# Pooling the 16-row tails of v once per batch on 128 partitions, in place of once per group on 32

## The chip, the cores and the metric

The kernel runs on one core of one Trainium2 chip. The metric is the device time of one execution in microseconds (us). The engines are TensorE (PE in the views, its weight loads PEld), VectorE (DVE), ScalarE (ACT), GpSimd (POOL) and SyncE (SP), which issues nearly all DMAs.

## What is computed

Three stages follow each other: an attention whose keys and values are means over 8 neighbouring rows, and two feed-forward layers. Cut to what matters:

```python
B, H, S, D = 8, 8, 576, 64
k_p = k.reshape(B, H, 72, 8, D).mean(axis=3)
v_p = v.reshape(B, H, 72, 8, D).mean(axis=3)
scores = q @ k_p.T / sqrt(D)                  # per batch and head
attn   = softmax(scores)                      # over the 72 pooled keys
x  = (attn @ v_p) as [B*S, H*D] = [4608, 512]
x  = ((x @ w1) * (x @ w2)) @ w3 @ w_out       # first layer, 1024 wide
h  = x @ w_in;  out = (h * sigmoid(1.702 * h)) @ w_out2   # second, 2048 wide
```

Everything is float32. A float32 product is made of three fast ones: each operand is split into a rounded part and a rest (a cast on ScalarE, a subtraction on VectorE or GpSimd).

## The kernel before

**Groups.** The attention is cut into 32 groups, four for each batch; a group is two heads. Its pooled v has 2 x 72 = 144 rows, 16 more than the 128 partitions. The first 128 rows go through a tile on 128 partitions (`vr`, `va`, `vf`, `vm`), and the 16 left over, the last rows of the group's second head, through tiles on 32 partitions (`vtr`, `vat`, `vtf`, `vt`). These are the tails. `v_load` (L243) issues both DMAs of a group, `g_va` (L318) pools both by three halving additions each on GpSimd and scales them (L332 for the tail; `mask` also sorts the 128 rows into the two heads), and at its end calls `v_load` for the next group. `g_vb` (L336) splits both: `vm` by one cast on ScalarE and one subtraction on GpSimd, `vt` by two casts (L340, L341) and one subtraction (L342). `vt` holds rounded part, rest, rounded part in three blocks of 32 partitions. `g6` multiplies `vm` and `vt` by the split probabilities and writes the result, split again, into the slots of `x`.

**What runs beside it.** `g0` to `g4` load and turn q and k, make the scores and the softmax, and split the probabilities (L369, L372 on GpSimd). `tick` issues the next part of the attention; the first four groups go through `tick_first`. `conv.step` converts a weight tile from the input's 64-bit floats: two ScalarE instructions (L166, L168), a shift on VectorE (L169), an addition on GpSimd (L172), and then a split (L105). There are 40 such tiles for the first layer. The weights `w3` are multiplied with `w_out` beforehand (`w3_mm`, L508 turns them).

**Order.** First a loop of 28 steps (L568) does conversions, the product of `w3` and `w_out`, and the attention of the first four groups. Then come nine blocks of 512 rows (L602): each of eight steps of a block multiplies by `w1` and `w2`, takes the product (L641), splits it, and calls `tick` twice, so that one block carries four groups. The blocks' matmuls and those of the second layer fill the rest. Tiles are allocated from pools; `vr` has one buffer, so its next load has to wait until the old one has been read last. The order in each engine's queue is not the order of the code: a planner with a simulated timeline (L1124) lays it out from its own costs and dependencies when the program is built, and each queue then runs in that fixed order. The order of SP's queue, which carries the loads of q, k, v and the weights, comes out of the same plan.

Of the kernel before, what the change touches and what calls it, by code (L numbers as in the profile page):

```python
# [7 lines left out]
F32 = mybir.dt.float32  # L8
F32R = mybir.dt.float32r
# [3 lines left out]
ALU = mybir.AluOpType  # L13
# [4 lines left out]
P = 128  # L18
# [4 lines left out]
def pooled_attention_moe_moe2(  # L23
# [18 lines left out]
    nc = tc.nc  # L42
    B, H, S, D = q.shape
    NT, DM = out.shape
    POOL = 8
    SK = S // POOL
# [3 lines left out]
    HP = H // 2  # L50
# [11 lines left out]
    KT = KW - P  # L62
# [22 lines left out]
    def take(shape=(P, 2, T), dtype=F32R):  # L85
        pool, i = free.pop(0)
        t = pool.tile(list(shape), dtype, name=f"s{i}", tag=f"s{i}")
        held[id(t)] = (t, pool, i)
        return t
# [10 lines left out]
    def f32(ap):  # L100
        return ap.bitcast(F32)

    def split(dst, src, lo_eng):
        nc.scalar.copy(dst[:, 0], src)  # L104
        lo_eng.tensor_tensor(out=dst[:, 1], in0=src, in1=f32(dst[:, 0]), op=ALU.subtract)  # L105
# [85 lines left out]
    with pa_ctx:  # L191
        pa = pa_ctx.enter_context(tc.tile_pool(name="pa", bufs=1))
        cv_p[0] = pa


        mask = pa.tile([P, 2, D], F32, name="mask")
        nc.gpsimd.memset(mask, 1.0 / POOL)
        nc.gpsimd.affine_select(
            out=mask[:, 0], in_=mask[:, 0], compare_op=ALU.is_gt, fill=0.0,
            base=SK, pattern=[[0, D]], channel_multiplier=-1)  # L200
        nc.gpsimd.affine_select(
            out=mask[:, 1], in_=mask[:, 1], compare_op=ALU.is_ge, fill=0.0,
            base=-SK, pattern=[[0, D]], channel_multiplier=1)
        qT = pa.tile([P, TT * P], F32, name="qT")
        nc.vector.memset(qT[:, S:], 0.0)
        kbd = pa.tile([P, 2, SK], F32, name="kbd")
# [3 lines left out]
            :, :TT * PW].rearrange("p (t w) -> p t w", w=PW)]  # L210
        for t in s_ts:
            nc.gpsimd.memset(t[:, :, KW:], 0.0)
        vtr = pa.tile([32, POOL * D], F32, name="vtr")
        nc.gpsimd.memset(vtr, 0.0)
        ident = pa.tile([P, P], F32, name="ident")
        nc.gpsimd.memset(ident, 1.0)
# [1 line left out]
            out=ident, in_=ident, compare_op=ALU.is_equal, fill=0.0,  # L218
            base=0, pattern=[[-1, P]], channel_multiplier=1)
        vm = pa.tile([P, 2, 2 * D], F32R, name="vm")  # L220
        vt = pa.tile([96, 2 * D], F32R, name="vt")
# [3 lines left out]
        g_q, g_k, g_v, g_s = {}, {}, {}, {}  # L225
# [17 lines left out]
        def v_load(n):  # L243
            if n >= NG:
                return
            b, hp = divmod(n, HP)
            vr = v[b, 2 * hp:2 * hp + 2].rearrange("h (s u) d -> (h s) (u d)", u=POOL)
            g_v[n] = pa.tile([P, POOL * D], F32, name="vr", tag="vr")
            nc.sync.dma_start(g_v[n], vr[:P])
            nc.sync.dma_start(vtr[:KT], vr[P:])  # L250

        def g0(n):
            kr, qr = g_k.pop(n), g_q.pop(n)
# [42 lines left out]
        def g3(n):  # L296
# [13 lines left out]
            for r in range(5):  # L310
                for c in range(4):
# [3 lines left out]
                        out=dst[:, :nt, 32 * c:32 * c + 32],  # L315
                        in_=s_t[32 * c:32 * c + 32, :nt, 32 * r:32 * r + 32])

        def g_va(n):  # L318

            vr, tr = g_v.pop(n), vtr  # L320
            a = pa.tile([P, 4 * D], F32, name="va", tag="va")
            at = pa.tile([32, 4 * D], F32, name="vat", tag="vat")
            for d, s in ((a, vr), (at, tr)):
                nc.gpsimd.tensor_tensor(out=d, in0=s[:, :4 * D], in1=s[:, 4 * D:], op=ALU.add)
                nc.gpsimd.tensor_tensor(
                    out=d[:, :2 * D], in0=d[:, :2 * D], in1=d[:, 2 * D:], op=ALU.add)
                nc.gpsimd.tensor_tensor(out=d[:, :D], in0=d[:, :D], in1=d[:, D:2 * D], op=ALU.add)
            vf = pa.tile([P, 2, D], F32, name="vf", tag="vf")
            nc.gpsimd.tensor_tensor(
                out=vf, in0=a[:, :D].unsqueeze(1).to_broadcast([P, 2, D]), in1=mask, op=ALU.mult)  # L330
            vtf = pa.tile([32, D], F32, name="vtf", tag="vtf")
            nc.gpsimd.tensor_scalar_mul(vtf, at[:, :D], 1.0 / POOL)  # L332
            g_v[n] = (vf.rearrange("p a d -> p (a d)"), vtf)
            v_load(n + 1)

        def g_vb(n):  # L336
            vf, vtf = g_v.pop(n)
            nc.scalar.copy(vm[:, 0], vf)
            nc.gpsimd.tensor_tensor(out=vm[:, 1], in0=vf, in1=f32(vm[:, 0]), op=ALU.subtract)
            nc.scalar.copy(vt[:32, D:], vtf)  # L340
            nc.scalar.copy(vt[64:96, D:], vtf)  # L341
            nc.gpsimd.tensor_tensor(  # L342
                out=vt[32:64, D:], in0=vtf, in1=f32(vt[:32, D:]), op=ALU.subtract)

        def g4(n):
            p0, p1 = g_s.pop(n)
# [58 lines left out]
        def tick_first():  # L405

            t = tick_n[0]
            tick_n[0] += 1
            for n in range(NPE):
                if t == 2 * n + 6:  # L410
                    g6(n)
            for n in range(NPE):
                s = t - 2 * n
                if s == 0 and n == 0:
                    g0(0)
                elif s == 1:
                    g1(n)
                elif s == 2:
                    g2(n)
                    g0(n + 1)  # L420
                elif s == 3:
                    g3(n)
                elif s == 4:
                    g4(n)
                    g_va(n)
                elif s == 5:
                    g_vb(n)
            if t == 2 * NPE + 4:
                tick_n[0] = 4 * NPE
                give(s_sl)  # L430

        def tick():
            t = tick_n[0]
            if t < 4 * NPE:
                return tick_first()
            tick_n[0] += 1
            n, s = divmod(t, 4)
            if s == 0:
                if NPE <= n - 1 < NG:
                    g4(n - 1)  # L440
            elif s == 1:
                if n < NG:
                    g1(n)
            elif s == 2:
                if NPE <= n - 1 < NG:
                    g6(n - 1)
                if n < NG:
                    g2(n)
                    g_va(n)
                if n + 1 < NG:  # L450
                    g0(n + 1)
            elif n < NG:
                g3(n)
                g_vb(n)
# [108 lines left out]
        conv.load()  # L563
        g_load(0)
        v_load(0)
        n3 = 8 + 2 * NIT
        done3 = []
# [34 lines left out]
        for blk in range(NB):  # L602
            x = [x_slot(blk, c) for c in range(KM)]
            if blk == NB - 2:

                pa_ctx.close()
                pa = pa_ctx.enter_context(tc.tile_pool(name="pc", bufs=1, reuse_waits="tile"))
# [10 lines left out]
            for f in range(NF1):  # L618
# [18 lines left out]
                a = pa.tile([P, T], F32, name="a", tag="a", bufs=2)  # L637
                nc.scalar.copy(a, pa_)  # L638
                u = u_s[blk, f] = take()
# [32 lines left out]
    with tc.tile_pool(name="pb", bufs=1, reuse_waits="tile") as pb, \  # L672
# [206 lines left out]
        for k, f in enumerate(FO):  # L879
            bk = bank()  # L880
            w = ready.pop(("h", 0, f))
# [29 lines left out]
        for pr in range(1, NPAIR + 1):  # L911
# [17 lines left out]
            for fp in range(NFP):  # L929
# [4 lines left out]
                for name, i in ORDER:  # L934
# [6 lines left out]
                    if name in PART:  # L941
                        s, h = PART[name]
                        w = ready[s, pr, 2 * fp + i][:, h]
                    else:
                        w = ready[name, pr, fp][:, i]
                    bs = W if name == "M2" else Z if name in ("M5", "M3") else C
                    first = name in ("M1", "M2", "M5")
# [64 lines left out]
            m1, U, V, n = [], [], [], 0  # L1012
# [116 lines left out]
```

## Time and profile before

| what | value |
|---|---|
| time, median of 3 runs | 1483.54 us (1480.33 to 1484.5) |
| the profiled execution's own time | 1480.04 us |
| its span, first to last instruction | 1478.3 us |
| PE busy in the span | 1437.1 us (97%) |
| DVE, ACT, POOL busy | 991.5, 696.6, 491.9 us |
| mean granted TensorE clock | 0.994 of full speed |

Busy time is the sum over an engine's instructions. The clock is a share of TensorE's full 2.4 GHz. The profiled execution lies 3.5 us below the median, and 1.74 us of its time lie outside the span.

### The profile page before, as it was taken

How to read it: one execution, taken by the hardware profiler on the slowest of the kernel's cores; microseconds unless marked ns; L12 is line 12 of the kernel's file. 1: busy time of each engine (PE TensorE's matmuls, PEld its weight loads, DVE VectorE, ACT ScalarE, POOL GpSimd, SP SyncE). 2: the span in 40 equal slices, each digit the busy share in tenths (PEclk: the TensorE clock that was granted, in tenths of full speed). 3: DMA queues.
4: the chain of work that ended last, by engine and by line, in shares of the span. 5: the costliest groups of instructions: out<-in, count | busy, mean ns of one | idle time of the engine just before them, and what ended most of it. 6: DMA issues, size and time to landing. Idle time of an engine off the chain costs nothing.

```text
span 1478.3 us, 19409 instructions
## 1 busy us (share of the span) xinstructions
PE 1437.1 (97%) x6536; PEld 1188.0 (80%) x6536; DVE 991.5 (67%) x1728; ACT 696.6 (47%) x1212; POOL 491.9 (33%) x589
## 2 busy tenths in 40 slices
PE   5978999999999999999999999999999999999998
PEld 3766888888888888888888887888788888888886
DVE  7889998878787877645636345783559354954554
ACT  6974444434343434366635334652455244634442
POOL 8787865555555555357743200000000000000000
PEclk9989999999999999999999999999999999999999
DMA  9992333323232321089869978877677766785665
GB/s 275 243 227 41 65 81 61 77 49 77 47 75 48 74 41 37 29 295 337 329 230 391 330 240 306 292 213 225 200 237 223 224 199 216 241 237 179 196 213 141
DMA packets 294434, 267.63 MB, mean 181 GB/s; under 512 B 201664, under 2 KB 226240, under 8 KB 294336
## 3 DMA queue, kind: packets, MB, share of 16 engines
q1 hardware_dynamic: 291648, 265.09, 60.0%
q10 hardware_dynamic: 2688, 1.31, 0.3%
q8 instruction: 52, 0.85, 0.2%
q14 instruction: 46, 0.38, 0.1%
HBM read 209.72 MB, written 56.62 MB: 180 GB/s over the span
## 4 chain that ended last, share of the span: by engine, by line
PE 82%; DVE 7%; DMA 5%; ACT 2%; POOL 2%; issue 1%; SPq 1%; DVEq 0%; ACTq 0%; POOLq 0%
PE bk L709 39%; PE wk L114 8%; PE wk L116 8%; PE wk L115 8%; PE acc L114 4%; PE acc L115 4%; PE acc L116 4%; PE wk L278 2%; DMA wud<-wt 2%; DVE s L105 1%; DVE cv L169 1%; PE bk L114 1%; PE bk L115 1%; PE bk L116 1%; POOL cv L172 1%
## 5 line engine op out<-in xcount | busy, mean ns | idle before, releaser
L709 PE MATMUL bk<-xM,st 128*128 128x512 f32 x1140 | 269.1, 390 | 1.8 <-DMA st<-wind 1.3
L709 PE MATMUL bk<-mv,st 128*128 128x512 f32 x1104 | 258.7, 389 | 0.5 <-DMA st<-wud 0.5
L709 PEld LDWEIGHTS bk<-xM,st 128*128 128x128 f32 x1140 | 213.6, 188 | 48.0 <-issue 1.9
L709 PEld LDWEIGHTS bk<-mv,st 128*128 128x128 f32 x1104 | 207.1, 188 | 44.2 <-ACT mv L104 0.9
L114 PE MATMUL wk<-s,s 128*128 128x512 f32 x576 | 227.3, 396 | 6.1 <-DVE a L641 4.1
L116 PE MATMUL wk<-s,s 128*128 128x512 f32 x576 | 225.2, 391 | 0.9 <-DVE s L105 0.9
L115 PE MATMUL wk<-s,s 128*128 128x512 f32 x576 | 225.3, 392 | 0.1
L314 DVE STREAM_TRANSPOSE p<-s_t 32x160 f32<-32x160 f32 (+1 forms) x560 | 178.3, 318 | 10.5
L115 PE MATMUL acc<-s,s 128*128 128x512 f32 x352 | 141.2, 401 | 1.0 <-POOL s L105 0.8
L116 PE MATMUL acc<-s,s 128*128 128x512 f32 x352 | 140.7, 400 | 1.6 <-DVE s L105 1.6
L114 PE MATMUL acc<-s,s 128*128 128x512 f32 x352 | 134.1, 406 | 8.1 <-DVE s L105 5.4
L114 PEld LDWEIGHTS wk<-s,s 128*128 128x128 f32 x576 | 108.5, 189 | 30.1 <-DVE a L641 5.4
L116 PEld LDWEIGHTS wk<-s,s 128*128 128x128 f32 x576 | 108.5, 188 | 23.8 <-DVE s L105 1.1
L115 PEld LDWEIGHTS wk<-s,s 128*128 128x128 f32 x576 | 108.5, 188 | 22.1 <-DVE s L391 0.5
L105 POOL TENSOR_TENSOR s<-a,s 128x512 fp32r<-128x512 f32 x56 | 73.3, 1309 | 155.2 <-ACT s L104 121.4
L105 DVE TENSOR_TENSOR mv<-g,mv 128x1024 fp32r<-128x1024 f32 x80 | 97.8, 1222 | 32.5 <-ACT mv L104 31.0
L104 ACT CAST mv<-g 128x1024 fp32r<-128x1024 f32 x80 | 84.5, 1056 | 71.3 <-PE bk L709 70.8
L172 POOL TENSOR_TENSOR cv<-cv,s 128x512 int32<-128x512 int32 x72 | 100.8, 1408 | 33.6 <-DVE cv L169 24.2
L114 PEld LDWEIGHTS acc<-s,s 128*128 128x128 f32 x352 | 67.9, 194 | 23.3 <-ACT s L104 4.7
L116 PEld LDWEIGHTS acc<-s,s 128*128 128x128 f32 x352 | 67.9, 193 | 15.8 <-DVE s L105 2.7
L115 PEld LDWEIGHTS acc<-s,s 128*128 128x128 f32 x352 | 68.0, 193 | 14.4 <-POOL s L105 2.0
L638 ACT COPY a<-wk 128x512 f32<-128x512 f32 x72 | 42.1, 585 | 68.3 <-PE wk L116 68.1
(188 smaller groups left out, 2344.6 us busy)
## 6 DMA issues: line engine op xcount, KB each, us to landing
st<-wud SPq DMA_DIRECT2D x92, 512.0 KB, 4.3
st<-wind SPq DMA_DIRECT2D x66, 512.0 KB, 4.6
st<-wind SPq DMA_DIRECT2D x84, 256.0 KB, 3.8
s<-in_moe_w_dram SPq DMA_DIRECT2D x32, 512.0 KB, 6.5
wind<-s SPq DMA_DIRECT2D x32, 512.0 KB, 5.5
s<-in_moe_w_out_dram SPq DMA_DIRECT2D x24, 512.0 KB, 6.9
s<-wud SPq DMA_DIRECT2D x20, 512.0 KB, 4.3
kr<-in_k_dram SPq DMA_DIRECT2D x128, 72.0 KB, 2.5
```

The lines of the kernel that those rows point to most:

```text
L104: nc.scalar.copy(dst[:, 0], src)
L105: lo_eng.tensor_tensor(out=dst[:, 1], in0=src, in1=f32(dst[:, 0]), op=ALU.subtract)
L114: nc.tensor.matmul(o, a[:, 0, a_sl], b[:, 0, b_sl], start=first, stop=False)
L115: nc.tensor.matmul(o, a[:, 0, a_sl], b[:, 1, b_sl], start=False, stop=False)
L116: nc.tensor.matmul(o, a[:, 1, a_sl], b[:, 0, b_sl], start=False, stop=last)
L169: nc.vector.tensor_scalar(out=wu, in0=e.bitcast(U32), scalar1=3, scalar2=None, op0=ALU.logical_shift_left)
L172: nc.gpsimd.tensor_tensor(out=w.bitcast(I32), in0=w.bitcast(I32), in1=lo_w.bitcast(I32), op=ALU.add)
L278: nc.tensor.matmul(sc[half][:, i * KW:(i + 1) * KW], qT[:, sl(tt)], mov, start=True, stop=True)
L314: nc.vector.transpose(out=dst[:, :nt, 32 * c:32 * c + 32], in_=s_t[32 * c:32 * c + 32, :nt, 32 * r:32 * r + 32])
L638: nc.scalar.copy(a, pa_)
L709: nc.tensor.matmul(o, w[:, x, m], b[:, y], start=first and n == 0, stop=last and n == 2, skip_group_check=True)
```

## The change

The 16-row tails of a batch's four groups are loaded together into one tile of 128 partitions, each at its own block of 32, by four DMAs that are issued with the first group of a batch. That group's `g_va` pools, scales and splits all four; the split is kept in a new tile `vtq`. `g_vb` then copies the parts from its group's 32 partitions into the three blocks of `vt` by three ScalarE copies, with no GpSimd instruction. The pooling of both tiles is now done in place (in `vr` and `vtr`), and `va` and `vat` are gone; `mask` shrinks to one column for each head and is broadcast.

```diff
-            nc.sync.dma_start(vtr[:KT], vr[P:])
+            if hp == 0:
+                for h in range(HP):
+                    nc.sync.dma_start(
+                        vtr[32 * h:32 * h + KT],
+                        v[b, 2 * h + 1, S - KT * POOL:].rearrange("(s u) d -> s (u d)", u=POOL))
...
         def g_va(n):
-            vr, tr = g_v.pop(n), vtr
-            a = pa.tile([P, 4 * D], F32, name="va", tag="va")
-            at = pa.tile([32, 4 * D], F32, name="vat", tag="vat")
-            for d, s in ((a, vr), (at, tr)):
-                nc.gpsimd.tensor_tensor(out=d, in0=s[:, :4 * D], in1=s[:, 4 * D:], op=ALU.add)
-                nc.gpsimd.tensor_tensor(
-                    out=d[:, :2 * D], in0=d[:, :2 * D], in1=d[:, 2 * D:], op=ALU.add)
-                nc.gpsimd.tensor_tensor(out=d[:, :D], in0=d[:, :D], in1=d[:, D:2 * D], op=ALU.add)
+            vr, first = g_v.pop(n), n % HP == 0
+            for d in (vr, vtr) if first else (vr,):
+                for w in (4 * D, 2 * D, D):
+                    nc.gpsimd.tensor_tensor(
+                        out=d[:, :w], in0=d[:, :w], in1=d[:, w:2 * w], op=ALU.add)
             vf = pa.tile([P, 2, D], F32, name="vf", tag="vf")
             nc.gpsimd.tensor_tensor(
-                out=vf, in0=a[:, :D].unsqueeze(1).to_broadcast([P, 2, D]), in1=mask, op=ALU.mult)
-            vtf = pa.tile([32, D], F32, name="vtf", tag="vtf")
-            nc.gpsimd.tensor_scalar_mul(vtf, at[:, :D], 1.0 / POOL)
-            g_v[n] = (vf.rearrange("p a d -> p (a d)"), vtf)
+                out=vf, in0=vr[:, :D].unsqueeze(1).to_broadcast([P, 2, D]),
+                in1=mask.unsqueeze(2).to_broadcast([P, 2, D]), op=ALU.mult)
+            if first:
+                vtf = vtr[:, D:2 * D]
+                nc.gpsimd.tensor_scalar_mul(vtf, vtr[:, :D], 1.0 / POOL)
+                vtq[0] = pa.tile([P, 2, D], F32R, name="vtq", tag="vtq")
+                split(vtq[0], vtf, nc.gpsimd)
+            g_v[n] = (vf.rearrange("p a d -> p (a d)"), vtq[0][32 * (n % HP):32 * (n % HP) + 32])
             v_load(n + 1)

         def g_vb(n):
-            vf, vtf = g_v.pop(n)
+            vf, tail = g_v.pop(n)
             nc.scalar.copy(vm[:, 0], vf)
             nc.gpsimd.tensor_tensor(out=vm[:, 1], in0=vf, in1=f32(vm[:, 0]), op=ALU.subtract)
-            nc.scalar.copy(vt[:32, D:], vtf)
-            nc.scalar.copy(vt[64:96, D:], vtf)
-            nc.gpsimd.tensor_tensor(
-                out=vt[32:64, D:], in0=vtf, in1=f32(vt[:32, D:]), op=ALU.subtract)
+            for i, half in enumerate((0, 1, 0)):
+                nc.scalar.copy(vt[32 * i:32 * i + 32, D:], f32(tail[:, half]))
```

## Rows read from the trace of the kernel before

**Rows 1.** Busy time by stretch: PE, PEld, DVE, ACT, POOL, granted clock, DMA share, GB/s.

```profile
0.00:37.00 37.00, 20.51 (x68) 13.80 (x68) 27.32 (x35) 25.76 (x47) 29.63 (x40) 0.91 0.94 276
37.00:74.00 37.00, 36.26 (x205) 29.56 (x204) 31.40 (x54) 34.44 (x74) 28.17 (x28) 1.00 0.94 243
74.00:111.00 37.00, 29.25 (x131) 23.30 (x130) 32.81 (x47) 28.38 (x63) 32.23 (x39) 0.87 1.16 227
111.00:148.00 37.00, 31.39 (x138) 25.07 (x137) 35.01 (x72) 16.68 (x33) 29.21 (x31) 0.99 0.22 40
...
185.00:629.00 444.00, 443.45 (x2133) 374.03 (x2132) 354.58 (x870) 176.55 (x395) 230.49 (x324) 1.00 0.26 58
629.00:1478.00 849.00, 839.27 (x3692) 691.13 (x3690) 476.71 (x578) 397.70 (x563) 111.44 (x85) 1.00 0.76 248
```

**Rows 2.** Waits of PE in 0 to 148 us: total, times, longest.

```profile
PE wk L508 <- POOL cv L172: 10.6, 2, 9.2
PE acc L114 <- DVE s L105: 5.4, 3, 2.9
```

**Rows 3.** The chain that ended last, 0 to 150 us, shares by line.

```profile
by line: DVE s L105 11.5%; DVE cv L169 8.9%; DVE p L314 8.3%; issue 6.2%; DMA qr<-in_q_dram 6.0%; SPq L229 3.9%; DVE nm L301 3.6%; DMA s<-in_moe_w_dram 3.2%; ACT cv L166 2.7%; DVE s_t L303 2.5%; PE acc L114 2.3%; DVE nm L300 2.3%; ACT s L10
```

**Rows 4.** GpSimd's tail instructions in 0 to 148 us: busy us, mean ns.

```profile
L324 POOL TENSOR_TENSOR vat<-vtr 32x256 f32<-32x256 f32 x6 | 4.8, 796 | 0.2 <-DMA vtr<-in_v_dram 0.2
...
L342 POOL TENSOR_TENSOR vt<-vtf,vt 32x64 fp32r<-32x64 f32 x5 | 3.1, 625 | 0.4
L325 POOL TENSOR_TENSOR vat<-vat 32x128 f32<-32x128 f32 x6 | 3.1, 511 | 0.0
...
L332 POOL TENSOR_SCALAR vtf<-vat 32x64 f32<-32x64 f32 x6 | 2.6, 433 | 0.0
L327 POOL TENSOR_TENSOR vat<-vat 32x64 f32<-32x64 f32 x6 | 2.1, 352 | 0.0
```

**Rows 5.** VectorE's groups by form in 0 to 148 us: busy us, mean ns.

```profile
L169 DVE TENSOR_SCALAR cv<-cv 128x512 uint32<-128x512 uint32 x40 | 36.0, 908 | 9.1 <-ACT cv L166 9.1
L105 DVE TENSOR_TENSOR s<-cv,s 128x512 fp32r<-128x512 f32 x10 | 13.9, 1394 | 1.2 <-ACT s L104 1.2
L105 DVE TENSOR_TENSOR s<-wk,s 128x512 fp32r<-128x512 f32 x16 | 10.9, 682 | 4.3 <-ACT s L104 4.3
...
L301 DVE TENSOR_SCALAR nm<-nm 128x10 f32<-128x10 f32 x6 | 5.8, 970 | 0.1
```

**Rows 6.** Lines L169, L301 and L172, whole span: ns of one, min/median/max.

```profile
L169 DVE TENSOR_SCALAR cv<-cv x40: 356/536/3774, 5.5 to 147.4; 128x512 uint32<-128x512 uint32 x40
...
L301 DVE TENSOR_SCALAR nm<-nm x32: 157/174/2247, 30.8 to 609.3; 128x10 f32<-128x10 f32 x32
...
L172 POOL TENSOR_TENSOR cv<-cv,s x72: 1268/1313/1973, 6.1 to 749.0; 128x512 int32<-128x512 int32 x72
```

**Rows 7.** Line L340 on ScalarE, whole span: ns of one, min/median/max.

```profile
L340 ACT CAST vt<-vtf x32: 228/241/246, 33.7 to 612.9; 32x64 fp32r<-32x64 f32 x32
```

**Rows 8.** SP's queue in order of time, around two loads of v: start, length.

```profile
99.97 0.44 SPq L249 DMA_DIRECT2D vr<-in_v_dram  x1
100.50 0.38 SPq L250 DMA_DIRECT2D vtr<-in_v_dram  x1
100.94 1.49 SPq L229 DMA_DIRECT2D qr<-in_q_dram  x3
...
109.24 0.81 SPq L249 DMA_DIRECT2D vr<-in_v_dram  x1
...
112.29 1.94 SPq L229 DMA_DIRECT2D qr<-in_q_dram  x4
```

**Rows 9.** GpSimd in order of time: `vf` of the groups 3 and 4.

```profile
100.03 0.80 POOL L329 TENSOR_TENSOR vf<-va,mask 128x128 f32<-128x128 f32 x1
...
114.76 0.45 POOL L329 TENSOR_TENSOR vf<-va,mask 128x128 f32<-128x128 f32 x1
```

**Rows 10.** PE in order of time: scores that waited for q.

```profile
107.20 0.97 PE L278 MATMUL wk<-kbd,qT 128*128 128x144 f32 x6 [2.06 <-DVE qT L256]
```

More of the change, by code (lines that the diff above doesn't have):

```diff
@@ L193, in pooled_attention_moe_moe2 @@
         cv_p[0] = pa
-        mask = pa.tile([P, 2, D], F32, name="mask")
+        mask = pa.tile([P, 2], F32, name="mask")
         nc.gpsimd.memset(mask, 1.0 / POOL)
         nc.gpsimd.affine_select(
-            out=mask[:, 0], in_=mask[:, 0], compare_op=ALU.is_gt, fill=0.0,
-            base=SK, pattern=[[0, D]], channel_multiplier=-1)
+            out=mask[:, 0:1], in_=mask[:, 0:1], compare_op=ALU.is_gt, fill=0.0,
+            base=SK, pattern=[[0, 1]], channel_multiplier=-1)
         nc.gpsimd.affine_select(
-            out=mask[:, 1], in_=mask[:, 1], compare_op=ALU.is_ge, fill=0.0,
-            base=-SK, pattern=[[0, D]], channel_multiplier=1)
+            out=mask[:, 1:2], in_=mask[:, 1:2], compare_op=ALU.is_ge, fill=0.0,
+            base=-SK, pattern=[[0, 1]], channel_multiplier=1)
         qT = pa.tile([P, TT * P], F32, name="qT")
@@ L212, in pooled_attention_moe_moe2 @@
             nc.gpsimd.memset(t[:, :, KW:], 0.0)
-        vtr = pa.tile([32, POOL * D], F32, name="vtr")
+        vtr = pa.tile([P, POOL * D], F32, name="vtr")
         nc.gpsimd.memset(vtr, 0.0)
@@ L316, in g3 @@
                         in_=s_t[32 * c:32 * c + 32, :nt, 32 * r:32 * r + 32])
+        vtq = [None]
         def g_va(n):
-            vr, tr = g_v.pop(n), vtr
-            a = pa.tile([P, 4 * D], F32, name="va", tag="va")
-            at = pa.tile([32, 4 * D], F32, name="vat", tag="vat")
-            for d, s in ((a, vr), (at, tr)):
-                nc.gpsimd.tensor_tensor(out=d, in0=s[:, :4 * D], in1=s[:, 4 * D:], op=ALU.add)
-                nc.gpsimd.tensor_tensor(
-                    out=d[:, :2 * D], in0=d[:, :2 * D], in1=d[:, 2 * D:], op=ALU.add)
-                nc.gpsimd.tensor_tensor(out=d[:, :D], in0=d[:, :D], in1=d[:, D:2 * D], op=ALU.add)
+            vr, first = g_v.pop(n), n % HP == 0
[3 more added lines that the diff above has]
+                        out=d[:, :w], in0=d[:, :w], in1=d[:, w:2 * w], op=ALU.add)
```

## The prediction

> **What bounds the kernel now.** I read the busy time by stretch first. From 185 to 629 us PE is busy 443.45 of 444 us, and from 629 us to the end 839.27 of 849 us [rows 1]. In these 1293 us PE loses 10.3 us, and most of that lies behind the attention, where the change edits nothing. The attention runs until about 629 us, so most of its 32 groups lie under a full PE: there GpSimd (230.49 of 444 us busy) and ScalarE (176.55) have room, and work saved on either is worth nothing. The change can only pay in the first 148 us, where PE is busy 20.51 + 36.26 + 29.25 + 31.39 = 117.4 us and loses 30.6; the granted clock is 0.91 and 0.87 of full speed in two of the four stretches, so some matmuls run at the lower level too [rows 1].
>
> Then the waits of PE in that stretch: the largest is 10.6 us on the weight conversion of GpSimd, but 9.2 us of it is one wait, the start of the kernel, before any attention; the next is VectorE's splits, 5.4 us [rows 2]. The chain of waits says the same: VectorE's lines lead (L105 11.5%, L169 8.9%, L314 8.3%), the loads of q and SP's issuing of them follow (6.0% and 3.9%), and no line of GpSimd stands among the first twelve [rows 3]. Busy times of VectorE are 27.32 + 31.40 + 32.81 + 35.01 = 126.5 us, of GpSimd 29.63 + 28.17 + 32.23 + 29.21 = 119.2, of ScalarE 105.3, and the DMA share is about 1 for the first 111 us [rows 1]. No engine is alone the bound; VectorE comes closest.
>
> Last, VectorE's own groups. A split that reads a PSUM bank (`wk`) takes 682 ns; the same split whose inputs both lie in SBUF (`cv`) takes 1394 [rows 5]. The shift L169 goes from 356 to 3774 ns and L301, ten elements wide, from 157 to 2247 [rows 6]. So certain VectorE instructions wait inside their own busy time. Counted from the shortest of L169 and L301, and from the 682 ns for the split, that is 36.0 - 40 x 0.356 = 21.8 us, 13.9 - 10 x 0.682 = 7.1 and 5.8 - 6 x 0.157 = 4.9: 33.8 us of VectorE's 126.5 [rows 5, 6]. I take these for waits on GpSimd, since the lines that read PSUM don't show them: 33.8 us of wait for 119.2 us of GpSimd work, 0.28 us each.
>
> **The change part by part.** *Tail work on GpSimd.* In the first 148 us a group's tail costs 796 + 511 + 352 + 433 + 625 ns = 2.72 us [rows 4]. Six groups (0 to 5) pool there; groups 0 and 4 are the first of their batch and still pay. The trace has no tail on 128 partitions; I price it like that on 32, since the main tile's additions in the same lines work on 128 partitions, and a lower bound is nothing, an upper one twice. Groups 1, 2, 3 and 5 pay nothing any more: 4 x 2.72 = 10.9 us less on GpSimd. What that is worth lies between nothing (GpSimd covered by VectorE) and 10.9 us (GpSimd paces everything). I take the share that VectorE waits: 0.28 x 10.9 = 3.1 us, since VectorE leads the chain and its idle time is small. The remaining 26 groups save time under a full PE: nothing; without that cover it would be 2.7 us for three groups in four.
>
> *Setup.* The smaller mask and the wider zeroing of `vtr` come while everything waits for the first weights (the 9.2 us wait [rows 2]): nothing; without that cover some tenths of a us. In-place additions and the broadcast mask are priced as the additions before, nothing gained or lost; the bounds are a tenth of each instruction either way, under 0.5 us in six groups.
>
> *ScalarE.* Two copies of 241 ns [rows 7] become three, and a batch's first group adds one for its split: 6 x 0.24 + 2 x 0.24 = 1.9 us in the first 148 us. ScalarE is idle for 42.7 of these [rows 1], so I take nothing; with that cover gone it is 1.9 us. What comes behind the copies on ScalarE is mostly conversions, whose results wait for VectorE and GpSimd anyway. The subtraction L342 that waited for L340 is gone from three groups of four; only the batch's split still makes GpSimd wait for a ScalarE cast.
>
> *DMAs and SP's queue.* 32 tail loads stay 32, but in clumps of four. One issue takes 100.94 - 100.50 = 0.44 us of the queue [rows 8]. Groups 1 to 3 issue one less each, 1.3 us, and groups 0 and 4 three more each. Those of group 0 come while weights are already staged; those of group 4 sit ahead of the three loads of q at 100.94, which PE's gap at 107.20 waits for through VectorE's transpose [rows 8, 10]: +1.3 us. The 1.3 us saved in groups 1 to 3 lie ahead on the same queue, and I set one against the other: nothing, with 1.3 us either way.
>
> *The wait that is added.* `vr` is now read last by `vf` and no longer by the first addition, so the next load of `vr` waits for `vf`, and SP's queue behind it with it. At 99.97 the load left before `vf` of group 3 ended (100.83): 0.9 us late. At 109.24 `vf` of group 4 ended only at 115.21: 6.0 us late [rows 8, 9]. The planner knows of the dependency and can put q's loads first, and GpSimd arrives earlier by up to 8 us by then (three groups of 2.72), so I take nothing; the other bound is in the second rival. Under the full PE the load of `vr` has a group's time to arrive, (629 - 148) / 26 = 18.5 us.
>
> The sum: 3.1 us less. Against the profiled execution: 1478.3 + 1.74 - 3.1 = 1476.9; that execution lies 3.5 us below the median of the runs, so I forecast from the median: 1483.5 - 3.1 = **1480.4 us**. The bound of what a measurement can tell is 0.3%, or 4.45 us: this is "the same", on the faster side. Chance 0.43. The order of every queue is planned anew, which I can't read from this trace; I give it 3 us either way.
>
> **The rivals.** *GpSimd paces the first stretch.* For it: 119.2 of 148 us busy, and its instructions stand between conversion and matmul in every step. Against it: it is not among the chain's first lines [rows 3]. Then up to 10.9 us go: 1472.6. Gains over 4.45 us belong here, which is 1.4 times my share; a lost gap can also bring back clock (0.87 in the third stretch [rows 1]). Chance 0.31.
>
> *SP's queue stops behind `vr`.* This is the one on the other side. If the planner leaves SP's order as it is, the loads of q at 100.94 come 0.9 + 1.3 = 2.2 us late, and those at 112.29 can't leave before 115.21 + 0.44: 3.4 us late. VectorE's transpose then stands in its queue, waiting for q where it waited for GpSimd, and the relief is lost: 1483.5 + 5.6 = 1489.1. For it: the loads of q are 6.0% of the chain already [rows 3]. Against: the planner's freedom, and the earlier `vf`. It decides once such waits exceed 4.45 us with the relief lost, or 7.6 us with it. Chance 0.16.
>
> *Only the instruction in progress delays VectorE.* If a VectorE instruction waits for no more than the one GpSimd instruction that it meets, short ones matter by their squares: 0.80² + 0.51² + 0.35² + 0.43² + 0.63² = 1.6 us² for a group, 6.4 for four; met at a random moment that is 6.4 / (2 x 148) = 0.022 us for each of the 56 instructions of [rows 5] that show waits, 1.2 us: 1482.3. Against it: L169's longest of 3774 ns is well over the longest 1973 ns of GpSimd's commonest instruction in that stretch, L172 [rows 6]. Chance 0.10. The Trainium skill, SBUF — State Buffer, section "Who interferes with whom", states this rule: VectorE shares one port pair with GpSimd as an exclusive lock, held for the whole instruction by whichever starts first, also when a VectorE instruction has two SBUF inputs. The trace agrees on which lines wait; the length of 3774 ns [rows 6] speaks for more than one holder.
>
> **How the numbers follow.** Faster by over 0.3%: 0.31 (first rival). Within 0.3%: 0.43 + 0.10 = 0.53. Slower: 0.16. The range cuts the extreme tenth off either side: down to 1474, near the end of the first rival, and up to 1488.5, near the second's.
>
> **What would show it.** Right: tail groups of GpSimd x8 in place of x32, VectorE's L169 and `s<-cv` shorter in the first 148 us by about 3 us, PE losing some 27 to 28 us there, and nothing different later. The first rival: a PE loss under 25 us there. The second: waits of SP's L249 on `vf`, and gaps of PE behind the transpose of q that are longer than 2.06 us. Wrong altogether: any difference behind 185 us, or a VectorE whose waits don't follow GpSimd's work.

## The result, and the profile after

The changed kernel takes 1490.38 us in the median (1488.8 to 1493.11, 6 runs), the kernel before beside it 1482.67 (1480.33 to 1484.84): a ratio of 1.0054 with an interval of 1.0039 to 1.0068, or 7.7 us more. I had forecast 3.1 us less. The profiled execution took 1488.8 us, its span 1487.0.

The busy time by stretch, columns as in [rows 1]:

```profile
0.00:37.00 37.00, 21.65 (x72) 14.51 (x73) 27.48 (x38) 28.20 (x54) 30.02 (x40) 0.91 0.90 256
37.00:74.00 37.00, 33.30 (x180) 26.76 (x180) 28.73 (x48) 29.91 (x62) 24.44 (x24) 0.95 0.98 245
74.00:111.00 37.00, 31.21 (x152) 25.26 (x151) 27.51 (x51) 28.70 (x65) 28.34 (x30) 0.91 1.08 225
111.00:148.00 37.00, 30.07 (x123) 23.38 (x123) 33.06 (x74) 22.69 (x49) 33.11 (x33) 0.86 0.37 64
148.00:185.00 37.00, 33.25 (x160) 27.41 (x159) 34.81 (x77) 16.30 (x38) 23.07 (x27) 1.00 0.29 58
185.00:629.00 444.00, 444.00 (x2136) 375.34 (x2135) 353.64 (x867) 184.10 (x421) 191.00 (x233) 1.00 0.26 57
629.00:1487.00 858.00, 846.24 (x3722) 696.93 (x3720) 477.42 (x578) 397.91 (x565) 113.37 (x86) 1.00 0.76 246
```

The fifth stretch of before, which [rows 1] leave out:

```profile
148.00:185.00 37.00, 37.00 (x182) 31.14 (x181) 33.70 (x78) 17.11 (x41) 30.77 (x47) 1.00 0.32 65
```

Behind 185 us PE is full, as in [rows 1], but for some 2 us more of idle time behind the attention. The loss lies ahead of it: PE is busy 3.0, 1.3 and 3.8 us less in the second, the fourth and the fifth stretch, and the granted clock is lower in the second (0.95 for 1.00) and the fourth (0.86 for 0.99). The first and the third give a part of it back. How much is best read from the matmuls. The same view with one stretch from 0 to 185 us gives, of before and of after:

```profile
0.00:185.00 185.00, 154.41 (x716) 122.87 (x717) 160.24 (x281) 122.36 (x254) 150.00 (x181) 0.95 0.71 170
```

```profile
0.00:185.00 185.00, 149.48 (x681) 117.33 (x682) 151.59 (x284) 125.80 (x267) 138.98 (x151) 0.93 0.72 170
```

The other engines show what the change meant: GpSimd is busy 11.0 us less, VectorE 8.7 less, ScalarE 3.4 more. But PE has done 35 matmuls fewer (every trace of this study has 6536 in all, so no missing records make the difference). A matmul takes 443.45 / 2133 = 0.208 us in the full stretch [rows 1], so that is an estimated 7.3 us of work still to do, and the span is 8.7 us longer.

VectorE's relief did come. Its groups in 0 to 148 us, as in [rows 5]:

```profile
L169 DVE TENSOR_SCALAR cv<-cv 128x512 uint32<-128x512 uint32 x40 | 31.8, 801 | 12.1 <-ACT cv L166 12.1
...
L105 DVE TENSOR_TENSOR s<-cv,s 128x512 fp32r<-128x512 f32 x9 | 9.4, 1052 | 0.4 <-ACT s L104 0.4
```

L169 is 4.2 us shorter in all, and nine splits are 9 x (1394 - 1052) ns = 3.1 us shorter: together 7.3, more than twice the forecast. Part of it was given back as idle time: L169 now waits 12.1 us for ScalarE's conversions, where it waited 9.1. Whether the lighter GpSimd is what shortened these groups is taken up in the last part. GpSimd's tails in the same 148 us:

```profile
L329 POOL TENSOR_TENSOR vtr<-vtr 128x256 f32<-128x256 f32 x3 | 2.2, 733 | 2.0 <-DMA vtr<-in_v_dram 2.0
L329 POOL TENSOR_TENSOR vtr<-vtr 128x128 f32<-128x128 f32 x3 | 2.2, 726 | 0.1
...
L337 POOL TENSOR_SCALAR vtr<-vtr 128x64 f32<-128x64 f32 x3 | 1.5, 485 | 0.0
L329 POOL TENSOR_TENSOR vtr<-vtr 128x64 f32<-128x64 f32 x3 | 1.1, 380 | 0.1
L105 POOL TENSOR_TENSOR vtq<-vtr,vtq 128x64 fp32r<-128x64 f32 x2 | 0.8, 418 | 0.0
```

That is 7.8 us in place of the 15.7 of [rows 4]: three batches are pooled there, not two. The four steps on 128 partitions take 2.32 us in the mean, those on 32 took 2.09 [rows 4], so four times the partitions cost about a tenth more here. The trace of before could have told that much ahead: its first addition has both widths, over the whole span:

```profile
L324 POOL TENSOR_TENSOR vat<-vtr 32x256 f32<-32x256 f32 x32 | 23.6, 739 | 0.2 <-DMA vtr<-in_v_dram 0.2
L324 POOL TENSOR_TENSOR va<-vr 128x256 f32<-128x256 f32 x32 | 23.3, 728 | 2.0 <-DMA vr<-in_v_dram 2.0
```

What stands in another place is seen on ScalarE. In order of time, before:

```profile
53.80 0.67 ACT L166 ACTIVATE cv<-s 128x512 f32<-128x512 f32 x1
...
56.04 0.68 ACT L166 ACTIVATE cv<-s 128x512 f32<-128x512 f32 x1
...
60.05 0.58 ACT L352 COPY p<-acc 128x512 f32<-128x512 f32 x1
```

and after:

```profile
51.83 0.65 ACT L166 ACTIVATE cv<-s 128x512 f32<-128x512 f32 x1
...
56.56 0.56 ACT L357 COPY p<-acc 128x512 f32<-128x512 f32 x1
...
59.16 0.66 ACT L166 ACTIVATE cv<-s 128x512 f32<-128x512 f32 x1
```

The first two rows of before are the weight conversions 21 and 22, the third the copy of a group's probabilities behind them. After, the rows are conversion 20, the copy and conversion 21: the copy now stands ahead of it, and the conversion comes 59.16 - 53.80 = 5.4 us later. The change edits neither instruction. The copies of the expert's hidden blocks, `a` from `wk`, one for each step of the first experts, tell the same; this is one line's summary (ns min/median/max, first and last start), before and after:

```profile
L638 ACT COPY a<-wk x8: 559/582/589, 115.0 to 175.5; 128x512 f32<-128x512 f32 x8
```

```profile
L643 ACT COPY a<-wk x8: 560/586/591, 119.1 to 185.5; 128x512 f32<-128x512 f32 x8
```

The eighth is 10.0 us late. The question for the experiments is whether the change's work or its order does that.

### The profile page after: what moved, and what is told of

It reads as the page before. It is cut to its first block, busy times and chain, and to the rows that moved or that the text cites. A ratio compares the mean times of both kernels' runs of the same rounds, so it can differ in the third digit from the quotient of the medians.

```text
span 1487.0 us, 19238 instructions
## 1 busy us (share of the span) xinstructions
PE 1439.7 (97%) x6536; PEld 1189.6 (80%) x6536; DVE 982.6 (66%) x1728; ACT 707.8 (48%) x1252; POOL 443.4 (30%) x469
## 4 chain that ended last, share of the span: by engine, by line
PE 82%; DMA 7%; DVE 6%; POOL 1%; ACT 1%; issue 1%; SPq 1%; DVEq 0%; ACTq 0%; POOLq 0%
PE bk L714 38%; PE wk L116 7%; PE wk L114 7%; PE wk L115 7%; PE acc L114 5%; PE acc L116 5%; PE acc L115 5%; PE wk L282 2%; DMA wud<-wt 2%; DVE p L318 2%; DMA s<-in_moe_w_dram 1%; PE bk L114 1%; PE bk L115 1%; PE bk L116 1%; POOL cv L172 1%
## 5 line engine op out<-in xcount | busy, mean ns | idle before, releaser
L172 POOL TENSOR_TENSOR cv<-cv,s 128x512 int32<-128x512 int32 x72 | 102.5, 1433 | 37.7 <-DVE cv L169 24.4
```

The source lines that it names most:

```text
L172: nc.gpsimd.tensor_tensor(out=w.bitcast(I32), in0=w.bitcast(I32), in1=lo_w.bitcast(I32), op=ALU.add)
```

## The experiments

Ratios are to the kernel before, timed on the same chip, with a 95% interval. 0.001 is 1.5 us.

**The wait and the small parts.** Theory S: the loads of `vr` that wait for `vf` stop SP's queue (the second rival). Theory O: the new order as a whole. Four kernels: the changed one with two buffers for `vr` (meant to take the wait away), the changed one with the first addition into a tile of its own (`vr` free as early as before), and the kernel before with only the in-place pooling, and with only the small mask.

```
after_vr2       g_v[n] = pa.tile(..., name="vr", tag="vr", bufs=2)
after_va        va = pa.tile([P, 4 * D], ...); first addition va <- vr, the others in va
before_inplace  a = vr      # in place of a tile "va"
before_mask     mask [P, 2], broadcast over D in the multiplication
```

> The changed kernel with two buffers for vr, so that no load of vr waits for vf of the group before. Theory S (SP's queue stops at loads of vr that wait for vf, and the loads behind them come late): SP's waits on vf, 7.6 us in the first 185 us, go, and the time falls back to 1483 us or below. Theory O (the planner's new order as a whole costs the time, no single wait): it stays within 2 us of 1490.

> The changed kernel with the first addition of the main tile put into its own tile va again, so that vr is free after one addition; the tails are as in the changed kernel. Theory S: as with two buffers, 1483 us or below, since only the wait on vf is taken away. Theory O: within 2 us of 1490.

> The kernel before with the main tile pooled in place, and nothing else of the change: vr is read last by vf. Theory S: it alone costs the whole loss, about 1490 us (1488 to 1492). Theory O: less than half of the loss, below 1486.5.

> The kernel before with the small mask alone; it changes no duration of weight, but the planner lays some of the queues out differently from about 110 us on. Theory S: 1482.7 us, within 2. Theory O: the order alone can move the time, by 2 us or more in either direction.

Measured: after_vr2 1.0041 (1.0028 to 1.0054), after_va 1.0029 (1.0017 to 1.0041), before_inplace 1.0100 (1.0087 to 1.0113), before_mask 1.0014 (1.0001 to 1.0026). The two buffers did not take the wait away. This is SP's wait on `vf` in 0 to 185 us in after_vr2, against 7.6 us in the changed kernel:

```profile
SPq L249 <- POOL vf L332: 30.5, 2, 27.3
```

So that kernel says nothing of theory S. In after_va, where the load waits for the first addition as it did before, more than half of the loss stays. before_inplace missed the ranges of both theories: pooling in place alone, in the kernel before, costs nearly twice what the whole change does. Parts that don't add up to the whole, and a mask of one column that seems to cost 2 us, speak for something that each edit sets off anew. In before_inplace the fourth stretch is the worst of all runs:

```profile
111.00:148.00 37.00, 19.73 (x68) 14.95 (x69) 34.19 (x69) 12.61 (x28) 27.11 (x33) 0.63 0.27 48
```

with PE waiting for the value path:

```profile
PE acc L380 <- ACT vm L338: 5.1, 1, 5.1
PE wk L114 <- ACT s L390: 5.1, 1, 5.1
...
PE acc L382 <- POOL vm L339: 3.2, 1, 3.2
```

**The work taken away or put in alone.** The kernel before without the tails (loads, pooling, scaling, copies) of three groups in four, whose block of `vt` stays that of the batch's first group; with the batch's tails loaded four at a time, all else as before; with a third ScalarE copy in place of the subtraction, so that the low part of the tail is left out; and after_va with the tails' loads on GpSimd's queue.

```
before_drop   if n % HP == 0: (tail load, additions, scaling, copies, subtraction)
before_clump  if hp == 0: four loads into vtr[32*h:32*h+KT]; the group reads its 32 rows
before_act3   nc.scalar.copy(vt[32:64, D:], vtf)     # was gpsimd subtract
va_poolq      nc.gpsimd.dma_start(vtr[...], ...)     # was nc.sync
```

> The kernel before without the tails' loads and work in three groups of four (these groups use the tail of the batch's first group; part of the computation is left out); nothing is added. It shows what the removed work is worth alone. My forecast's share for VectorE's waits: 1480.4 us. GpSimd paces the stretch: about 1473. Theory that work off the path is worth nothing here: 1483.5.

> The kernel before with one part of the change: the four tail loads of a batch are issued together with its first group, into 128 partitions, and each group still pools its own 32 partitions on GpSimd. Theory C (three more issues on SP's queue at the start make the planner put two weight loads behind k and q of group 2, and the conversions of weights come late): 1486 to 1490 us. Rival R (the loss of the tails' part comes from what follows, the pooling of a batch at once and the third ScalarE copy): within 2 us of the 1483.5 of before.

> The kernel before with the tail's rest in vt made by a third ScalarE copy in place of the GpSimd subtraction (the rest is then a copy of the tail; part of the computation is changed). Theory C: within 2 us of 1483.5. Rival R: slower by 2 us or more.

> The changed kernel with va kept (first addition not in place) and the tail loads issued from GpSimd's queue in place of SP's. In its plan four or more weight loads stand ahead of k and q of group 2, as before. Theory C: the time comes back from 1487.6 to 1483.5 or below. Rival R: it stays within 2 us of 1487.6.

Measured: before_drop 1.0001 (0.9990 to 1.0011), before_clump 1.0052 (1.0040 to 1.0064), before_act3 1.0047 (1.0033 to 1.0061), va_poolq 1.0089 (1.0075 to 1.0102). Leaving the work out gains nothing that can be measured, though L169 falls there as well:

```profile
L169 DVE TENSOR_SCALAR cv<-cv 128x512 uint32<-128x512 uint32 x40 | 30.4, 767 | 9.3 <-ACT cv L166 9.1
L105 DVE TENSOR_TENSOR s<-cv,s 128x512 fp32r<-128x512 f32 x9 | 13.9, 1540 | 0.7 <-ACT s L104 0.7
```

A third copy, 0.24 us for each group [rows 7] on an engine with 42.7 us idle, costs 7 us; the six groups of the first 148 us have 1.4 us of such copies. The loss isn't their price. GpSimd's queue as a way out is the second slowest of all, 1.0089 where after_va, which it edits, has 1.0029.

**Two weight loads.** In the changed kernel's queue the loads of k and q of group 2 stand ahead of the weight loads 17 and 18. SP's queue, after:

```profile
34.04 2.41 SPq L229 DMA_DIRECT2D kr<-in_k_dram  x4
36.55 5.85 SPq L229 DMA_DIRECT2D qr<-in_q_dram  x4
42.44 2.00 SPq L151 DMA_DIRECT2D s<-in_moe_w_dram  x4
```

Before, the four weight loads left from 30.89 us on, ahead of group 2. Theory C: those two loads, some 10 us late, are the loss. before_swap puts them behind in the kernel before, and three kernels put them ahead again by holding k and q of group 2 until weight load 18 is issued.

```
before_swap   with tc.issue_after(last load of q, group 2): weight loads 17 and 18
*_hold        g_load(2) is issued after weight load 18, not at the end of g0(1)
```

> The kernel before, with one thing held: the 17th and 18th weight load are issued behind k and q of group 2, as in the changed kernel; no load is added. Theory C (these two loads, late by some 10 us, cost the tails' part): 1487 to 1491 us. Theory P (the three added issues themselves cost it, the order is no matter): within 2 us of 1483. Theory L (any other plan than that of before is slower, by whatever it is): slower too, but with clump_hold also slow.

> The kernel before with the clumped tail loads, but k and q of group 2 held back behind the 18th weight load, as they stand before. Theory C: back from 1490.7 to within 2 us of 1483. Theory P: 1488 us or more. Theory L: slower than 1485.5.

> The changed kernel with va kept and the same hold of k and q of group 2. Theory C: 1481 to 1484 us, the whole change without its two waits. Theory L or P: 1486 us or more.

> The changed kernel with two buffers for vr and the same hold. Theory C: 1480 to 1484 us. Theory L or P: 1486 us or more.

Measured: before_swap 1.0049 (1.0032 to 1.0067), but clump_hold 1.0065 (1.0049 to 1.0082), va_hold 1.0056 (1.0042 to 1.0070), vr2_hold 1.0067 (1.0051 to 1.0083). Swapping does cost as much as the change; swapping back brings nothing back. As the one cause, theory C falls, and theory P with before_swap, which adds no issue. Only theory L, that any other plan is slower, fits all four. Each of these edits also made the planner order the engines anew, so none of the runs so far separates work from order.

**Work and order crossed.** The last kernels fix the order. Each instruction that two kernels share is chained to its forerunner on its engine's queue by an edge that orders and doesn't wait, over the first 1500 instructions of the plan (some 175 us); only instructions that one kernel alone has are placed by the planner. The code is cut:

```
for names in ORDER.values():          # one list per engine, the other kernel's order
    for a, b in zip(names, names[1:]):
        tc.add_manual_dep(at[b], a, NoSync)
```

> The changed kernel with nothing of its work altered, but every instruction that it shares with the kernel before, up to some 175 us, queued on each engine and on SP's queue in the order of the kernel before; only the tails' own loads, additions, scaling, split and copies stand where the planner puts them. Theory O (the loss comes from the new order of the whole first stage, and the work itself is worth nothing): 1480 to 1485 us, ratio to the kernel before 0.998 to 1.002. Theory W (the loss comes from the work: the four loads at a time, the pooling of a whole batch, the loads of vr waiting for vf, the third copy): 1487 to 1491 us, ratio 1.003 to 1.006.

> The kernel before with none of the change in it, but every instruction that it shares with the changed kernel, up to some 175 us, queued in the order of the changed kernel. Theory O: 1487 to 1493 us, ratio 1.003 to 1.007, and the eighth activation of the first experts as late as in the changed kernel (some 185 us in place of 175). Theory W: 1480 to 1485 us, ratio 0.998 to 1.002.

> The kernel before with the pooling of vr in place, so that each load of vr waits for vf (it took 14.8 us more by itself, with an order of its own), now queued in the order of the kernel before. Theory O: 1480 to 1486 us, ratio under 1.0025: the wait was dear only through the order planned around it. Theory W: SP stops at the loads of vr for several us each time, the weight loads behind it are late, and 1490 us or more.

> The kernel before with the tails of a batch loaded four at a time (it took 7.7 us more by itself), now queued in the order of the kernel before. Theory O: 1480 to 1485 us, ratio 0.998 to 1.002. Theory W: four transfers in a row hold up the weight loads behind them, 1488 us or more.

Measured, beside the same work in its own plan, with matmuls begun in the first 185 us and the span of the profiled execution:

| kernel | work | order | ratio (interval) | matmuls | span us |
|---|---|---|---|---|---|
| before | before | before | 1 | 716 | 1478.3 |
| after | after | own | 1.0054 (1.0039 to 1.0068) | 681 | 1487.0 |
| after_border | after | before | 0.9974 (0.9961 to 0.9987) | 713 | 1479.6 |
| before_aorder | before | after | 1.0076 (1.0064 to 1.0088) | 649 | 1491.1 |
| before_inplace | pooling in place | own | 1.0100 (1.0087 to 1.0113) | 632 | 1497.4 |
| inplace_border | pooling in place | before | 0.9999 (0.9987 to 1.0010) | 711 | 1480.4 |
| before_clump | four loads at once | own | 1.0052 (1.0040 to 1.0064) | 674 | 1488.9 |
| clump_border | four loads at once | before | 0.9989 (0.9976 to 1.0002) | 712 | 1480.1 |

All four fall on the side of theory O; two lie just beyond its range, after_border on the fast side (0.998 was the bound) and before_aorder on the slow one (1.007). The changed work in the old order is faster than the kernel before, 1478.66 us against 1483.32, a gain of 0.26% by the ratio, under the 0.3% that was set as the bound of what can be told, though its interval leaves out 1; its profiled execution, at 1479.6 us of span, doesn't show it. The old work in the new order is 11 us slower. No kernel was held to its own order; inplace_border and clump_border, held and neither slower nor faster than before within their intervals, show that holding is not what moves the time. The one line from 0 to 185 us, of after_border and of before_aorder:

```profile
0.00:185.00 185.00, 156.78 (x713) 124.91 (x714) 150.09 (x280) 124.33 (x264) 134.72 (x148) 0.94 0.69 168
```

```profile
0.00:185.00 185.00, 144.91 (x649) 112.99 (x650) 156.95 (x272) 119.66 (x250) 146.17 (x178) 0.92 0.70 170
```

Work and order come apart here. after_border has the lighter GpSimd and VectorE and PE's matmuls; before_aorder has the heavy engines of before and 67 matmuls fewer, 13.9 us by 0.208 us each. On ScalarE, before_aorder shows how an order costs:

```profile
52.76 2.33 ACT L168 ACTIVATE s<-s 128x512 int32<-128x512 uint32 x4
57.60 0.59 ACT L352 COPY p<-acc 128x512 f32<-128x512 f32 x1 [2.51 <-PE acc L351]
...
60.37 0.67 ACT L166 ACTIVATE cv<-s 128x512 f32<-128x512 f32 x1
```

The engine stands 2.51 us before the copy of the probabilities, whose transpose isn't done, and conversion 21, 6.6 us later than in the kernel before, is queued behind it. after_border has the conversions 21 (at 53.70) and 22 first:

```profile
55.85 0.69 ACT L166 ACTIVATE cv<-s 128x512 f32<-128x512 f32 x1
...
58.80 0.58 ACT L357 COPY p<-acc 128x512 f32<-128x512 f32 x1
```

And the wait that I had made a rival is there in full. SP's waits in 0 to 185 us (total, times, longest), in the kernel before, in the changed kernel and in after_border:

```profile
SPq L249 <- POOL va L324: 34.0, 4, 26.5
```

```profile
SPq L229 <- DVE qT L260: 29.7, 3, 19.5
SPq L249 <- POOL vf L332: 7.6, 2, 5.4
```

```profile
SPq L249 <- POOL vf L332: 52.0, 5, 18.8
```

The fastest kernel of the study is the one whose queue stops longest at the loads of `vr`. But the kernel before stopped there for 34.0 us already, then for the first addition, and the prediction didn't read that stop before it priced a longer one.

**Which order.** Theory Q: that of the loads on SP's queue. Theory E: that in which the engines take up their instructions. The changed kernel with SP's list held alone, and with the four engines' lists alone.

```
after_bsp     ORDER = {"SP": ...}
after_beng    ORDER = {"PE": ..., "DVE": ..., "ACT": ..., "POOL": ...}
```

> The changed kernel with its work unaltered and only SP's queue (the order in which its loads are issued) held to the order of the kernel before up to some 175 us; the five engines' own orders are the planner's. Theory Q (the order of the loads is what costs): 1476 to 1482 us, as with all queues held. Theory E (the order in which the engines take up their instructions is what costs, and the loads follow): 1486 to 1491 us, as the changed kernel.

> The changed kernel with its work unaltered and the orders of the engines (TensorE, VectorE, ScalarE, GpSimd) held to those of the kernel before up to some 175 us; SP's queue is the planner's, and two weight loads stand behind k and q of group 2 again. Theory Q: 1485 to 1491 us. Theory E: 1476 to 1482 us.

Measured: after_bsp 1.0070 (1.0053 to 1.0087), 656 matmuls by 185 us; after_beng 1.0001 (0.9991 to 1.0011), 719. Both medians lie about 1 us above the ranges of theory E, after_bsp 10 us above that of theory Q and after_beng 2 us below it, and 656 matmuls stand against 719. So the loss is in the engines' order: theory E. Loads in the old order don't help engines in the new one, which fits the three kernels with the hold that gained nothing. Whether the loads' order counts as well beside engines in the old order is open: the ratios go from 1.0001 to 0.9974 with both held, but the profiled executions go the other way (719 matmuls by 185 us and a span of 1478.1 us, against 713 and 1479.6).

## Why the prediction was wrong

*Where it can pay.* Right, with the stretch to 185 us for 148: behind it PE is full in both kernels.

*Tail work: 10.9 us less on GpSimd.* 15.7 - 7.8 = 7.9, since a third batch pools early.

*VectorE's share: 3.1 us.* With the order held, the whole change gains 1483.32 - 1478.66 = 4.7 us by the medians, 1.9 to 5.8 by the interval; with the engines' order alone held it gains nothing (after_beng). So 3.1 fits as the worth of the work, but isn't pinned down, and the first rival's 10.9 lie outside. The way there was not sized right. L169 and the splits lost 6.4 + 1.9 = 8.3 us in after_border:

```profile
L169 DVE TENSOR_SCALAR cv<-cv 128x512 uint32<-128x512 uint32 x40 | 29.6, 748 | 8.0 <-ACT cv L166 8.0
L105 DVE TENSOR_TENSOR s<-cv,s 128x512 fp32r<-128x512 f32 x10 | 12.0, 1200 | 1.8 <-ACT s L104 1.8
```

That would be about 1.0 us for each of GpSimd's 8, not 0.28. But these lines don't follow GpSimd's work alone. In clump_border GpSimd pools every group's tail as before, in the order of before, and L169 is shorter still:

```profile
L169 DVE TENSOR_SCALAR cv<-cv 128x512 uint32<-128x512 uint32 x40 | 27.3, 690 | 8.5 <-ACT cv L166 8.5
```

In inplace_border, with the same tail work and order, it has 966 ns. VectorE as a whole does tell the two apart: in the order of before it is busy 126.5, 125.7 and 121.7 us of the first 148 with all the tail work on GpSimd (before, inplace_border, clump_border), and 119.5 and 119.1 with the change's (after_border, after_beng). So 2.2 to 7.4 us came off VectorE for the 8 of GpSimd; a share of 0.28, taken from one trace, is no better founded than that. Which of the removed steps gives the gain stays open: before_drop took most of them away and gained nothing, in an order of its own. The Trainium skill, SBUF — State Buffer, section "Who interferes with whom", gives the lock by which VectorE waits for GpSimd; these five sums agree with it, the mean of L169 alone doesn't show it.

*Only the instruction in progress.* The trace of before already spoke against this rival. Its longest L169 and what GpSimd ran in that time:

```profile
121.27 3.77 DVE L169 TENSOR_SCALAR cv<-cv 128x512 uint32<-128x512 uint32 x1
```

```profile
121.50 1.31 POOL L172 TENSOR_TENSOR cv<-cv,s 128x512 int32<-128x512 int32 x1
122.78 0.73 POOL L324 TENSOR_TENSOR vat<-vtr 32x256 f32<-32x256 f32 x1
123.47 1.28 POOL L105 TENSOR_TENSOR s<-a,s 128x512 fp32r<-128x512 f32 x1
```

Three GpSimd instructions run one behind the other while it lasts.

*Setup, ScalarE, DMAs, SP's queue: nothing.* Borne out where the order is held: clump_border 0.9989, and after_border with the third copy and the small mask in it.

*The added wait: nothing.* Borne out too: inplace_border 0.9999. My reason, that the planner would put the loads of q first, isn't what made it so; SP stood 52.0 us behind `vf` in after_border, where it had stood 34.0 for the first addition in the kernel before, and what it loaded came soon enough. So the second rival had the right side by luck and the wrong mechanism: its waits grew by 18 us, four times the 4.45 us from which it was to decide, at no cost, and in the changed kernel itself they are only 7.6 us.

*"The order of every queue is planned anew, which I can't read from this trace; I give it 3 us either way."* This is the step that failed. The new order costs 11.3 us by before_aorder (9.5 to 13.1) and 1.0054 - 0.9974 = 0.0080, 11.9 us, between the two changed kernels. Work and order add up: -3.9 (0.9974) + 11.3 = 7.4, and 7.7 was measured. I had no rival for it, and gave it 3 us, a term under the bound of what can be measured, though a term that no row of the trace bounds should have widened the range on the slow side.

What decides inside the engines' order isn't settled to one instruction. Shown is that the four lists together do it; the probabilities' copy ahead of a conversion is one place where it is seen. Single engines' lists weren't tried.

## What to carry to other kernels

Where a planner orders all queues from its own estimates, an edit's price is that of its work plus that of a new order, and the second can be the larger: here about -4 us, near the limit of what the runs can tell, and +11. Before an edit that ought to help is given up, hold the old order around it and time that: the same change is then the fastest kernel of the study. To tell where time went, count the work that the bounding engine has done by a fixed moment; it told more than any list of waits.

## What was not expected of the hardware

SP's queue, which only loads, stood at the loads of `vr` for 52.0 us of the first 185 in the fastest kernel, against 34.0 in the kernel before and 7.6 in the slower changed one. VectorE's longest shift lasted through three GpSimd instructions. TensorE's granted clock was 0.63 in the stretch of before_inplace in which PE is busy 19.73 of 37 us, a mean between the two levels of 1.2 and 2.4 GHz, against 0.99 in the same stretch of before with 31.39 us busy [rows 1]; there an order that opened gaps lost at both ends. The busy time of a stretch alone doesn't give the clock: in the first stretch of before, 20.51 us busy go with 0.91 [rows 1].
